# Gated recurrent attention with a small mixture of attention experts on one core: chunk 0's loads on two queues, zero products only at the start, a refitted order

## Chip, cores and metric

One core of a Trainium2 chip. The metric is the device time of one execution in microseconds (us); for the kernel before, the median of three runs is given. A difference within 0.2% (0.64 us) is about what a measurement of this kernel cannot tell from no change.

## What is computed

All inputs are float32: batch 4, 8 heads, 768 positions, head size 48, 4 experts of width 64.

```python
# stage 1, for every batch b and head h, over t:
state = alpha[t, :, None] * state + outer(k[t], v[t])    # 48 x 48
y[t] = q[t] @ state
# stage 2, x = y with the heads side by side, (4, 768, 384):
logits = x @ w_gate                                      # 4 experts, top 2, softmax over them
for e in range(4):
    q, k, v = x @ wq[e], x @ wk[e], x @ wv[e]
    a = causal_softmax(q @ k.T / sqrt(64))
    out += weight_of_expert_e * (a @ v @ wo[e])          # 0 where e is not chosen
```

## The kernel before

**Tiles and stages.** The positions of a batch are cut into 6 chunks of 128, so there are 24 chunks (n = 0 to 23); three chunks are a unit (u = 0 to 7), so a batch is two units. All 8 heads of a chunk are worked on together, as 4 pairs that lie on the 128 partitions.

For a chunk, VectorE first turns the decays into running products: `prep_r` (a scan and a reciprocal, operation `r`), `prep_c` (a second scan, `c`) and `prep_kq` (the multiplication of queries and keys by them, `kq`); GpSimd copies out the chunk's total decay (`e`). Chunk 0 is done in two pieces of two pairs each, so these carry a piece number: `r.0.0`, `r.0.1` and so on. TensorE then multiplies keys by queries (`gla_a`, L217, operation `a`), transposes the keys (`gla_t`, L234, `t`), forms the chunk's addition to the state (`gla_u`, L263, `u`) and the output (`gla_y`, L302, `y`), which sums the masked products of the chunk (`ms`) and the products with the state (`S`). Between them lie the mask (`m`, on VectorE L221, or on ScalarE L225 and GpSimd L229), the copies of the transposed keys (`kt`, `kr`, L238 or L240), and the state's own path: an addition on VectorE (L272), a scaling on GpSimd (L275) and the placing on ScalarE (L280).

For a unit, TensorE projects its 384 positions to queries and keys (`proj`, L325, `p`) and to values and gate logits (`vproj`, L351, `v`), forms scores (`score`, L400, `s`), transposes the weighted probabilities (`transp`, L452), multiplies them with the values (`av`, L477, `o`) and with `wo` (`outp`, L496, `w`). VectorE finds the maxima (L414, L407), ScalarE does the exponentials (L425), GpSimd the weighting (L437). Most matrices are split into a high and a low part, so that one product takes three passes (`xh` and `xl`, `wqkh` and `wqkl`). The low part of `wv` is made on TensorE by two products (L721, L722, operations `wx.v.0` and `wx.v.1`).

**What sets the order.** All instructions are written by a planner that runs while the kernel is built (`run`). It keeps a list of operations with what they depend on, the engines that may do them with an assumed duration each, the buffers they take, and a target time, which is a multiple of `PACE` (us for a chunk) with offsets from the table `OFF`. It goes through the engines in assumed time, takes for the engine that is next free the operation whose start and target are best (`PULL`, `HEAD`), and writes it down; the engines later run their instructions strictly in that order and wait on semaphores. `MARGIN` is added to the assumed time at which an input is there for TensorE. `FIRST` lists by hand the first operations of TensorE (P), VectorE (V), ScalarE (A) and GpSimd (G). `opening` issues the first loads and tells the planner when they are assumed to land (`arrive`, by `came`, from a rate and a lead).

**Zero products.** `warm` (L887) multiplies a constant tile with itself into an unused accumulator. `opening` writes four such products of 512 columns before any real work of TensorE. Later the planner writes more wherever it expects TensorE to be free for longer than `IDLE`:

```python
            if e == "P" and free["P"] > start and t - free["P"] > IDLE:
                x, i = min((s[0], i) for i, s in enumerate(slots["g"]) if s)
                k = int((t - max(x, free["P"]) - IDLE) / 0.11)
                if k > 0:
                    warm(i, k)
                    slots["g"][i] = [t, "P"]
```

The profile counts two records for each product of full-precision operands, such as these, those of L217, L263, L302 and L477, and one for each of the others.

**The first loads.** SyncE issues the decays of chunk 0 in two pieces (`load_al`, L118), ScalarE the queries and keys of chunk 0 in two pieces (`load_q`, L122); then SyncE issues the decays, queries and keys of chunks 1 and 2, the values, and the weights, in one long queue.

Of the kernel before, what the change touches and what calls it, by code (L numbers as in the profile page):

```python
# [17 lines left out]
B, H, S, D = 4, 8, 768, 48  # L18
# [8 lines left out]
P = 112  # L27
# [8 lines left out]
FIRST = dict(  # L36
    P="t.0 u.0 a.0 wx.v.0 a.1 t.1 wx.v.1 y.0 u.1",
    V="r.0.0 c.0.0 r.0.1 c.0.1 kq.0.0 kq.0.1 r.1.0 c.1.0 kq.1.0 r.2.0 m.1.1 m.1.0 S.1 c.2.0 kq.2.0 xl.0 sa.1 kt.2 xl.1 kr.2 m.2.1 m.2.0 r.3.0 c.3.0",
    A="kr.0 kt.0 wvh m.0.1 m.0.0 wl.v.0 kt.1 kr.1 B.1 wl.v.1 wqh.0 xh.0 xh.1 B.2 vo.0.0 wqh.1 xh.2 kt.3 vo.0.1 ph.0.0.0 ph.0.0.1 woh ck.0 vo.0.2 ck.2 kr.3 B.3",
    G="e.0.0 e.0.1 e.1.0 m.0.1 m.0.0")  # L40
RATE, LEAD = 377.0, 3.35
PACE = 12.4288
PULL = {"P": 0.0081, "V": 0.0044, "A": 0.0049, "G": 0.0171, "S": 0.0015}
SWITCH = 1.5202
# [5 lines left out]
CHANGE.update({(x, "f"): 0.2 for x in "asy"})  # L50
IDLE = 0.1929
SHARE = 0
HEAD = 0.012
MARGIN = 0.4162
SLOW = 1.1285
OFF = dict(load=2.5246, prep=0.6013, a=0.5833, y=-0.1718, p=0.0404, pw=0.5861, v=-0.6489, g=0.8219, s=-0.1513, step=0.9077, n=0.4583, tr=1.4644, o=1.0477, w=1.1357, wt=-1.0315, wv=-2.1607, hx=0.2944, hs=-1.4408, hp=1.0247, ck=0.1758, end=0.5579, hd=0.2767, sx=-0.9018, wo=-2.426, xo=0.3522, tk=-0.0639, kt=-0.2994, u=0.5172, m=-0.5537, ph=0.7581, vo=1.3685, to=0.0454, oh=-0.2153, rd=0.1911)
UNITS = dict(a=7, at=4, ms=2, kt=2, x=2, q=3, k=4, yy=2, vg=3, T=4, al=3, v=4, ot=2, st=2)
# [6 lines left out]
def tile_gla_moe(ctx: ExitStack, tc: tile.TileContext, qk_d, al_d, v_d, wqk_d, wv_d, wo_d, nat_d, vn_d, out_d):  # L64
# [486 lines left out]
    def chunk_ops(n):  # L551
# [12 lines left out]
        if not last:  # L564
            zt = (n - 1 + OFF["tk"] - head) * PACE
            op(("t", n), zt, [("kq", n, i) for i in range(len(pieces(n)))], [("P", 0.32, lambda: gla_t(n))], [("T", n)], [("pt", n), ("kt", n)], "t")
            zt += OFF["kt"] * PACE
            op(("kt", n), zt, [("t", n)], either(gla_k, 288, n), [("pt", n), ("kt", n)])
            op(("kr", n), zt, [("t", n)], either(gla_kr, 96, n), [("pt", n), ("kt", n)])
        z = (n + OFF["y"] - head) * PACE  # L570
# [5 lines left out]
        if not last:  # L576
            z = (n + OFF["u"] - head) * PACE
            op(("u", n), z, [("kt", n), ("kr", n), ("Lv", n)], [("P", 0.36, lambda: gla_u(n))], [("kt", n), ("v", n)], [("pu", n)], "y")
            nxt = [("e", n + 1, i) for i in range(len(pieces(n + 1)))]
            if n + 1 not in WHOLE:  # L580
                nxt.append(("cp", n + 1))
            z += (OFF["hs"] if n < HALF else OFF["sx"]) * PACE
            past = [("B", n - 1)] if n and c != 1 else []
            if c == 0:
                op(("S", n + 1), z, [("u", n)] + nxt + past, [("V", 0.37, lambda: state_first(n))], [("pu", n), ("T", n + 1)])
            else:
                op(("sa", n), z, [("u", n), ("S", n)], [("V", 0.37, lambda: state_add(n))], [("pu", n), ("st", n)], [("st", n)])
                op(("S", n + 1), z, [("sa", n)] + nxt + past, [("G", 0.6, lambda: state_scale(n))], [("st", n), ("T", n + 1)])
            op(("B", n + 1), z, [("S", n + 1)] + ([("y", n - 1)] if n else []), [("A", 0.62, lambda: state_place(n + 1))])

    def front_ops(u):
# [20 lines left out]
        back = [("g3", u - 1)] if u else []  # L612
        op(("g1", u), z, [("vo", u, 2)] + back, [("V", 0.87, lambda: gate_1(u))], [("vg", u)], lock=2)
        op(("g2", u), z, [("g1", u)], [("A", 0.21, lambda: gate_2(u))])
# [111 lines left out]
    def low_ops(name, z, done, w, high, low, n, wt):  # L726
        if name not in LOWS:
            f = lambda E: E.tensor_tensor(low, w, high.bitcast(F32), OP.subtract)
            op(("wl",) + name, z, [done], [("V", dv(n), lambda: f(V)), ("G", 0.12 + 0.0021 * n, lambda: f(G))], [wt], lock=True)
            return  # L730
# [36 lines left out]
    def run(start, arrive, busy):  # L767
# [37 lines left out]
        while todo:  # L805
# [86 lines left out]
    def opening():  # L892
# [26 lines left out]
        for n in (1, 2):  # L919
# [180 lines left out]
```

## Time and profile before

| | us |
|---|---|
| median of 3 runs (318.54 to 319.06) | 318.57 |
| the profiled execution | 318.76 |
| its span, first to last instruction | 317.0 |
| TensorE busy (weight loads beside it) | 308.2 (265.4) |
| VectorE busy | 249.5 |
| ScalarE busy | 208.9 |
| GpSimd busy | 128.2 |

The profiled execution is 1.76 us longer than its span and 0.19 us above the median. PE is TensorE, PEld its weight loads, DVE VectorE, ACT ScalarE, POOL GpSimd, SP SyncE; SPq and ACTq are the engines' DMA issues. A timeline row gives the start, the duration and the number of like instructions that follow each other; in brackets stands how long the engine was idle before and what ended that. The ends of matrix products are modelled, so the next product may start before the one ahead has ended; what an operation takes of TensorE's time is read from start to start. The granted clock is a share of 2.4 GHz, in the page's part 2 in tenths.

### The profile page before, as it was taken

The numbers are of one execution on the slowest core, as the hardware profiler recorded it, in microseconds if no ns is written. First come the engines' busy times: TensorE is split into PE (matmuls) and PEld (weight loads), VectorE is DVE, ScalarE is ACT, GpSimd is POOL, SyncE is SP. The second block draws the span as 40 slices with busy tenths as digits, with TensorE's granted clock in tenths as the row PEclk, the third lists the DMA queues.
The fourth block names the chain that finished last, engine by engine and source line by source line (L and its number), as shares of the span: only waits on it lengthen the run. The fifth ranks groups of instructions, "written<-read, shape, count | busy, mean of one in ns | idle before, by whom it ended". The sixth has DMA issues, their size and how long they took to land.

```text
span 317.0 us, 11044 instructions
## 1 busy us (share of the span) xinstructions
PE 308.2 (97%) x4410; PEld 265.4 (84%) x4410; DVE 249.5 (79%) x678; ACT 208.9 (66%) x588; POOL 128.2 (40%) x197
## 2 busy tenths in 40 slices
PE   8999999999999999999999999999999999999992
PEld 3699989898997979889997988889897988888692
DVE  5999899998999998898998989675865754487620
ACT  2464986796785868578775776655964765377841
POOL 6334137516463483526343226414280344033510
PEclk9999999999999999999999999999999999999998
DMA  7996275543526246524354334304100000102001
GB/s 246 389 377 192 70 233 184 156 125 93 158 71 193 84 108 179 146 66 119 106 170 94 117 84 153 90 8 136 41 2 2 3 2 25 53 0 77 2 30 60
DMA packets 26893, 35.21 MB, mean 111 GB/s; under 512 B 2288, under 2 KB 22864, under 8 KB 26832
## 3 DMA queue, kind: packets, MB, share of 16 engines
q1 hardware_dynamic: 26144, 33.69, 34.6%
q8 instruction: 37, 0.61, 0.8%
q10 hardware_dynamic: 688, 0.72, 0.7%
q14 instruction: 24, 0.20, 0.2%
HBM read 27.61 MB, written 4.72 MB: 102 GB/s over the span
## 4 chain that ended last, share of the span: by engine, by line
PE 95%; DMA 1%; DVE 1%; ACT 0%; issue 0%; ACTq 0%; DVEq 0%
PE g L325 16%; PE g L452 13%; PE g L477 12%; PE g L302 11%; PE g L400 11%; PE g L351 8%; PE g L496 8%; PE g L217 7%; PE g L887 3%; PE g L263 2%; PE g L234 2%; DMA at<-in_al_dram 1%; DVE at L178 1%; PE g L721 0%; DVE T L198 0%
## 5 line engine op out<-in xcount | busy, mean ns | idle before, releaser
L437 POOL TENSOR_SCALAR a<-a,cf,gw 128x128 f32<-128x128 f32 (+5 forms) x96 | 80.5, 851 | 71.4 <-DVE cf L431 45.5
L425 ACT ACTIVATE a<-a,mx 128x256 f32<-128x256 f32 (+3 forms) x96 | 51.5, 539 | 9.1 <-DVE mx L414 9.0
L452 PE MATMUL g<-ident,a 128*128 128x128 f32 x336 | 53.7, 277 | 0.0
L325 PE MATMUL g<-x,wqkh 128*128 128x384 f32 x192 | 51.7, 350 | 0.0
L229 POOL TENSOR_SCALAR_AFFINE_SELECT ms<-ms 128x512 f32<-128x512 f32 x31 | 22.1, 724 | 56.2 <-ACT ms L225 56.2
L452 PEld LDWEIGHTS g<-ident,a 128*128 128x128 f32 x336 | 39.7, 140 | 5.8 <-issue 2.3
L240 DVE COPY at<-g 128x512 f32<-128x512 f32 (+3 forms) x62 | 29.2, 479 | 16.9 <-PE g L452 15.9
L477 PE MATMUL g<-at,vg 128*32 128x384 f32 (+2 forms) x648 | 39.7, 389 | 0.0
L400 PE MATMUL g<-k,q 64*128 64x256 f32 (+3 forms) x384 | 39.2, 336 | 0.0
L238 ACT ACTIVATE at<-g 128x512 f32<-128x512 f32 (+3 forms) x66 | 30.4, 465 | 8.4 <-PE g L452 6.6
L477 PEld LDWEIGHTS g<-at,vg 128*32 128x32 f32 x648 | 19.3, 109 | 18.5 <-issue 15.3
L302 PE MATMUL g<-ms,v 128*32 128x128 f32 x768 | 33.0, 274 | 0.0
L325 PEld LDWEIGHTS g<-x,wqkh 128*128 128x128 f32 x192 | 33.0, 189 | 0.0
L400 PEld LDWEIGHTS g<-k,q 64*128 64x128 f32 x384 | 28.6, 185 | 5.2 <-issue 2.3
L325 PE MATMUL g<-x,wqkl 128*128 128x384 f32 x96 | 32.3, 337 | 0.0
L351 PE MATMUL g<-wvh,x 128*128 128x260 f32 x144 | 31.7, 296 | 0.0
L414 DVE CUSTOM_DVE_ANT_0 a<-g,cmask 128x128 f32<-128x128 f32 (+2 forms) x64 | 28.2, 483 | 2.0 <-PE g L400 1.8
L496 PE MATMUL g<-woh,yy 128*128 128x384 f32 x96 | 28.1, 351 | 0.0
L217 PE MATMUL g<-T 48*128 48x128 f32 x384 | 25.7, 275 | 0.0
L217 PEld LDWEIGHTS g<-T 48*128 48x128 f32 x384 | 24.0, 187 | 1.3 <-DVE T L198 0.4
L351 PEld LDWEIGHTS g<-wvh,x 128*128 128x128 f32 x144 | 24.0, 190 | 0.4 <-ACT ms L225 0.4
L302 PE MATMUL g<-T,S 112*32 112x128 f32 x480 | 24.2, 272 | 0.0
(113 smaller groups left out, 616.1 us busy)
## 6 DMA issues: line engine op xcount, KB each, us to landing
al<-in_al_dram SPq DMA_DIRECT2D x21, 387.0 KB, 3.9
T<-in_qk_dram SPq DMA_DIRECT2D x21, 384.0 KB, 4.2
v<-in_v_dram SPq DMA_DIRECT2D x24, 256.0 KB, 4.5
out_dram<-ot SPq DMA_DIRECT2D x23, 192.0 KB, 2.1
T<-T SPq DMA_DIRECT2D x42, 48.2 KB, 2.2
a<-in_al_dram SPq DMA_DIRECT2D x2, 516.0 KB, 6.7
T<-in_qk_dram SPq DMA_DIRECT2D x2, 512.0 KB, 7.1
at<-in_wqk_dram SPq DMA_DIRECT2D x1, 768.0 KB, 8.5
```

The lines of the kernel that those rows point to most:

```text
L217: PE.matmul(pa[s][:, C * p:C * p + C], t[r:r + D, p, C:2 * C], t[r:r + D, p, 0:C], start=True, stop=True, tile_position=(r, 0))
L238: A.activation(out, src, AF.Copy)
L240: V.tensor_copy(out, src)
L302: PE.matmul(o[32 * j:32 * j + 32, k], l, r, start=(i == 0), stop=(i == len(parts) - 1), tile_position=(0, 32 * j))
L325: PE.matmul(pj[:, :W3], w[:, kt, cs], x[:, kt, :], start=(i == 0), stop=(i == 8))
L351: PE.matmul(pv[:, 0:260], x[:, kt, 128 * i:128 * i + 128], w[:, kt, :], start=(m == 0), stop=(m == 8))
L400: PE.matmul(sc(u, pair, i, e, x, c1 - c0), q[r, i0, ts], k[r, i1, c0:c1], start=(y == 0), stop=(y == 2), tile_position=(64 * e, 0))
L425: A.activation(a[:, c0:c1], src, AF.Exp, bias=mx[:, 1:2], scale=-1.0 if last else 1.0, accum_out=sm[:, x:x + 1])
L437: G.tensor_scalar(a[:, 0:n], a[:, 0:n], CF[u % 2][:, 3 * pair + i, e:e + 1], gw[:, u, i, eg:eg + 1], op0=OP.mult, op1=OP.mult)
L452: PE.transpose(pt[:, 128 * (j - j0):128 * (j - j0) + 128], a[:, 128 * j:128 * j + 128], ident)
L477: PE.matmul(o[r:r + 32, lo:n1], v[:, j % 3, 64 * eg + x:64 * eg + x + 32], at(("at", u, pair, e))[:, min(j, 4), at_off(j) + lo:at_off(j) + ...
L496: PE.matmul(po[:, 0:DM], y[:, h, 128 * i:128 * i + 128], w[:, pair, :], start=(m == 0), stop=(m == 5))
```

## The change

1. The four loads of chunk 0 are issued ahead of all else, by ScalarE and SyncE in turn: decays piece 0 on ScalarE, piece 1 on SyncE, then queries and keys piece 0 on ScalarE, piece 1 on SyncE. The planner gets four fixed landing times for them in place of a rate.
2. The planner writes zero products only while its assumed time is below `START` = 27 and the assumed wait is over `IDLE` = 0.7; before, at any time and from 0.1929 on. The four products of `opening` stay.
3. Some assumed durations are corrected, and the planner's constants and the hand-written first order are set anew. What each instruction computes stays the same.

```diff
-    P="t.0 u.0 a.0 wx.v.0 a.1 t.1 wx.v.1 y.0 u.1",
-    V="r.0.0 c.0.0 r.0.1 c.0.1 kq.0.0 kq.0.1 r.1.0 c.1.0 kq.1.0 r.2.0 m.1.1 m.1.0 S.1 c.2.0 ...
+    P="a.0 t.0 u.0 wx.v.0 a.1",
+    V="r.0.0 r.0.1 c.0.0 kq.0.0 c.0.1 kq.0.1 r.1.0 c.1.0 kq.1.0 r.2.0 m.1.0 m.1.1 S.1 c.2.0 ...
...
-PACE = 12.4288
+PACE = 12.3704
...
-IDLE = 0.1929
+START = 27.0
+IDLE = 0.7
...
-MARGIN = 0.4162
+MARGIN = 0.4105
...
-            op(("kr", n), zt, [("t", n)], either(gla_kr, 96, n), [("pt", n), ("kt", n)])
+            op(("kr", n), zt, [("t", n)], either(gla_kr, 134, n), [("pt", n), ("kt", n)])
...
-                op(("S", n + 1), z, [("sa", n)] + nxt + past, [("G", 0.6, lambda: state_scale(n))], [("st", n), ("T", n + 1)])
-            op(("B", n + 1), z, [("S", n + 1)] + ([("y", n - 1)] if n else []), [("A", 0.62, lambda: state_place(n + 1))])
+                op(("S", n + 1), z, [("sa", n)] + nxt + past, [("G", 0.52, lambda: state_scale(n))], [("st", n), ("T", n + 1)])
+            op(("B", n + 1), z, [("S", n + 1)] + ([("y", n - 1)] if n else []), [("A", 0.75, lambda: state_place(n + 1))])
...
-            if e == "P" and free["P"] > start and t - free["P"] > IDLE:
+            if e == "P" and start < free["P"] < START and t - free["P"] > IDLE:
...
-        for i in (0, 1):
-            load_al(0, i, SY)
+        for load in (load_al, load_q):
+            for i, eng in enumerate((A, SY)):
+                load(0, i, eng)
         G.memset(ones, 1.0)
         A.activation(ones, ones, AF.Copy)
-        for i in (0, 1):
-            load_q(0, i, A)
...
-        for key, kb in (("La", 0, 0), 264), (("La", 0, 1), 264), (("Lq", 0, 0), 262), (("Lq", 0, 1), 262):
-            came(key, kb)
-        z[0] += 0.3
+        for key, us in (("La", 0, 0), 3.7), (("La", 0, 1), 4.7), (("Lq", 0, 0), 5.5), (("Lq", 0, 1), 6.2):
+            arrive[key] = (us, "S")
+        z[0] = 6.45
```

Two more assumed durations change in the same way (`gate_1` 0.87 to 0.96, the low parts of weights on GpSimd by 0.08), the whole table `OFF` and most of `PULL` get other numbers, and the first lists of ScalarE and GpSimd change in places. In the listings below the change's lines from 52 on are one higher than before, those of `opening` up to two.

TensorE at the start. `T_85` holds chunk 0's queries and keys, `v_92` its values, `kt_69` its transposed keys, `d1r` is the tile of the zero products. Before:

```order
L887 MATMUL g_108<-d1r 128x512 x4
L234 MATMUL g_101<-ident,T_85 128x128 x3
L887 MATMUL g_102<-d1r 128x512
L887 MATMUL g_102<-d1r 128x128
L263 MATMUL g_103<-v_92,kt_69 32x48 x3
```

In the change:

```order
L888 MATMUL g_108<-d1r 128x512 x4
L218 MATMUL g_101<-T_85 128x128
L218 MATMUL g_102<-T_85 128x128
L218 MATMUL g_101<-T_85 128x128
L218 MATMUL g_102<-T_85 128x128
L218 MATMUL g_101<-T_85 128x128
L218 MATMUL g_102<-T_85 128x128
L218 MATMUL g_101<-T_85 128x128
L218 MATMUL g_102<-T_85 128x128
L235 MATMUL g_103<-ident,T_85 128x128 x3
L888 MATMUL g_104<-d1r 128x384
L264 MATMUL g_105<-v_92,kt_69 32x48 x3
```

The products of keys and queries have moved ahead of the transposes, and the 640 columns of zeros behind the transposes are 384.

VectorE at the start (`at_63` holds chunk 0's decays, `a` those of chunk 1). Before:

```order
L178 SCALAR_TENSOR_TENSOR at_63<-at_63,d1r 128x258
L184 RECIPROCAL d1c_110<-at_63 128x2
L178 SCALAR_TENSOR_TENSOR at_63<-at_63,d1c_110 128x258
L178 SCALAR_TENSOR_TENSOR at_63<-at_63,d1r 128x258
L184 RECIPROCAL d1c_110<-at_63 128x2
L178 SCALAR_TENSOR_TENSOR at_63<-at_63,d1c_110 128x258
L198 TENSOR_TENSOR T_85<-T_85,at_63 128x2x2x128 x2
L178 SCALAR_TENSOR_TENSOR a<-a,d1r 128x516
```

In the change:

```order
L179 SCALAR_TENSOR_TENSOR at_63<-at_63,d1r 128x258
L185 RECIPROCAL d1c_110<-at_63 128x2
L179 SCALAR_TENSOR_TENSOR at_63<-at_63,d1r 128x258
L185 RECIPROCAL d1c_110<-at_63 128x2
L179 SCALAR_TENSOR_TENSOR at_63<-at_63,d1c_110 128x258
L199 TENSOR_TENSOR T_85<-T_85,at_63 128x2x2x128
L179 SCALAR_TENSOR_TENSOR at_63<-at_63,d1c_110 128x258
L199 TENSOR_TENSOR T_85<-T_85,at_63 128x2x2x128
L179 SCALAR_TENSOR_TENSOR a<-a,d1r 128x516
```

The same eight instructions stand ahead of chunk 1's first scan; the multiplication of the first piece has moved ahead of the second piece's second scan.

TensorE between the outputs of chunks 3 and 4 (`ms_67` and `ms_68` are their masked products, `S_114` and `S_115` their states). Before:

```order
L302 MATMUL g_104<-ms_67,v_92 32x128 x8
L302 MATMUL g_104<-T_85,S_114 32x128 x4
L887 MATMUL g_105<-d1r 128x448
L302 MATMUL g_106<-ms_68,v_93 32x128 x4
L302 MATMUL g_106<-T_86,S_115 32x128 x4
```

In the change:

```order
L303 MATMUL g_105<-ms_67,v_92 32x128 x8
L303 MATMUL g_105<-T_85,S_114 32x128 x4
L303 MATMUL g_107<-ms_68,v_93 32x128 x4
L303 MATMUL g_107<-T_86,S_115 32x128 x4
```

The 448 columns of zeros are gone. In all, 22 of the 27 zero products of the program are left out; TensorE's other products are the same in number and size, in an order that differs over the whole program. Apart from the zeros that order falls into 297 pieces of one kind each before (a piece being products of one kind that follow each other), and 292 now.

## Rows read from the trace of the kernel before

**Rows 1.** The page, parts 1 and 2: busy time by engine, granted clock in 40 slices.
```profile
PE 308.2 (97%) x4410; PEld 265.4 (84%) x4410; DVE 249.5 (79%) x678; ACT 208.9 (66%) x588; POOL 128.2 (40%) x197
...
PEclk9999999999999999999999999999999999999998
```

**Rows 2.** Waits of the whole run: who waited for whom, us in total, times, longest.
```profile
PE g L887 <- POOL d1r L151: 1.6, 1, 1.6
...
PE g L234 <- ACT ms L225: 0.4, 1, 0.4
```

**Rows 3.** Windows, all engines: stretch, its us, then busy us (x instructions) of each engine.
```profile
8.00:27.00 19.00, 18.25 (x344) 15.22 (x344) 18.18 (x27) 8.94 (x19) 7.56 (x10) 1.00 1.05 376
27.00:100.00 73.00, 72.59 (x1150) 64.61 (x1150) 67.06 (x176) 56.43 (x160) 33.00 (x48) 1.00 0.48 140
100.00:312.00 212.00, 210.92 (x2917) 183.03 (x2913) 160.18 (x470) 141.72 (x406) 82.18 (x113) 1.00 0.25 74
```

**Rows 4.** The same windows for line 887 (the zeros) alone.
```profile
8.00:27.00 19.00, 3.47 (x15) 2.23 (x14) 1.00 1.05 376
27.00:100.00 73.00, 3.35 (x12) 1.79 (x12) 1.00 0.48 140
100.00:312.00 212.00, 4.47 (x20) 3.05 (x20) 1.00 0.25 74
```

**Rows 5.** Timeline of TensorE, 41.6 to 46 us: start, us, engine, line, operation.
```profile
41.69 0.43 PE L887 MATMUL g<-d1r 128*128 128x64 f32 x2
41.93 0.37 PE L351 MATMUL g<-wvh,x 128*128 128x260 f32 x1
...
44.86 1.02 PE L887 MATMUL g<-d1r 128*128 128x448 f32 x2
45.81 0.42 PE L302 MATMUL g<-ms,v 128*32 128x128 f32 x8
```

**Rows 6.** Timeline of ScalarE, 44 to 45 us: the placing of a state.
```profile
44.35 0.73 ACT L280 ACTIVATE S<-sp 48x192 f32<-48x192 f32 x2
```

**Rows 7.** Timeline of the last unit, around 293 us.
```profile
293.01 0.86 ACT L238 ACTIVATE at<-g 128x512 f32<-128x512 f32 x2
...
293.11 0.81 PE L887 MATMUL g<-d1r 128*128 128x320 f32 x2
...
293.76 0.83 PE L452 MATMUL g<-ident,a 128*128 128x128 f32 x6
```

**Rows 8.** Timeline of the opening, 0 to 11 us.
```profile
1.58 6.42 PE L887 MATMUL g<-d1r 128*128 128x512 f32 x8 [1.58 <-POOL d1r L151]
...
4.74 0.70 DVE L178 TENSOR_TENSOR_SCAN at<-at,d1r 128x258 f32<-128x258 f32 x1 [2.73 <-DMA at<-in_al_dram]
...
7.84 1.27 DVE L198 TENSOR_TENSOR T<-T,at 128x512 f32<-128x512 f32 x2
...
8.61 0.88 PE L234 MATMUL g<-ident,T 128*128 128x128 f32 x3 [0.61 <-issue]
...
9.33 1.25 PE L887 MATMUL g<-d1r 128*128 128x512 f32 x4
...
10.50 0.54 PE L263 MATMUL g<-v,kt 128*32 128x48 f32 x32
```

**Rows 9.** DMA issues, 0.5 to 1.2 us: count, KB each, us from issue to landing.
```profile
at<-in_al_dram SPq DMA_DIRECT2D x1, 258.0 KB, 3.8
T<-in_qk_dram ACTq DMA_DIRECT2D x1, 256.0 KB, 2.7
```

**Rows 10.** DMA issue of chunk 2's decays, at 4.71 us.
```profile
a<-in_al_dram SPq DMA_DIRECT2D x1, 516.0 KB, 7.7
```

**Rows 11.** Timeline, 12.9 to 18.9 us: the chain of chunk 2.
```profile
12.91 1.66 DVE L178 TENSOR_TENSOR_SCAN a<-a,d1r 128x516 f32<-128x516 f32 x1
...
17.45 1.23 DVE L198 TENSOR_TENSOR T<-T,a 128x1024 f32<-128x1024 f32 x1
...
18.89 0.50 PE L234 MATMUL g<-ident,T 128*128 128x128 f32 x3
```

More of the change, by code (lines that the diff above doesn't have):

```diff
@@ L36 @@
 FIRST = dict(
-    P="t.0 u.0 a.0 wx.v.0 a.1 t.1 wx.v.1 y.0 u.1",
-    V="r.0.0 c.0.0 r.0.1 c.0.1 kq.0.0 kq.0.1 r.1.0 c.1.0 kq.1.0 r.2.0 m.1.1 m.1.0 S.1 c.2.0 kq.2.0 xl.0 sa.1 kt.2 xl.1 kr.2 m.2.1 m.2.0 r.3.0 c.3.0",
-    A="kr.0 kt.0 wvh m.0.1 m.0.0 wl.v.0 kt.1 kr.1 B.1 wl.v.1 wqh.0 xh.0 xh.1 B.2 vo.0.0 wqh.1 xh.2 kt.3 vo.0.1 ph.0.0.0 ph.0.0.1 woh ck.0 vo.0.2 ck.2 kr.3 B.3",
-    G="e.0.0 e.0.1 e.1.0 m.0.1 m.0.0")
+    P="a.0 t.0 u.0 wx.v.0 a.1",
+    V="r.0.0 r.0.1 c.0.0 kq.0.0 c.0.1 kq.0.1 r.1.0 c.1.0 kq.1.0 r.2.0 m.1.0 m.1.1 S.1 c.2.0 kq.2.0 xl.0 sa.1 kt.2 xl.1 kr.2 m.2.1 m.2.0 r.3.0",
+    A="kr.0 kt.0 wvh m.0.1 m.0.0 kr.1 wl.v.0 kt.1 B.1 xh.0 wl.v.1 wqh.0 xh.1 B.2 wqh.1 vo.0.0 xh.2 kt.3 vo.0.1 ph.0.0.0 ph.0.0.1 woh vo.0.2 ck.0 ck.2 ck.1 B.3 kr.3",
+    G="e.0.1 e.0.0 e.1.0 m.0.1 m.0.0")
 RATE, LEAD = 377.0, 3.35
-PACE = 12.4288
-PULL = {"P": 0.0081, "V": 0.0044, "A": 0.0049, "G": 0.0171, "S": 0.0015}
+PACE = 12.3704
+PULL = {"P": 0.0081, "V": 0.0043, "A": 0.0032, "G": 0.0196, "S": 0.001}
 SWITCH = 1.5202
@@ L50 @@
 CHANGE.update({(x, "f"): 0.2 for x in "asy"})
-IDLE = 0.1929
+START = 27.0
+IDLE = 0.7
 SHARE = 0
-HEAD = 0.012
-MARGIN = 0.4162
+HEAD = 0.0115
+MARGIN = 0.4105
 SLOW = 1.1285
-OFF = dict(load=2.5246, prep=0.6013, a=0.5833, y=-0.1718, p=0.0404, pw=0.5861, v=-0.6489, g=0.8219, s=-0.1513, step=0.9077, n=0.4583, tr=1.4644, o=1.0477, w=1.1357, wt=-1.0315, wv=-2.1607, hx=0.2944, hs=-1.4408, hp=1.0247, ck=0.1758, end=0.5579, hd=0.2767, sx=-0.9018, wo=-2.426, xo=0.3522, tk=-0.0639, kt=-0.2994, u=0.5172, m=-0.5537, ph=0.7581, vo=1.3685, to=0.0454, oh=-0.2153, rd=0.1911)
+OFF = dict(load=2.4221, prep=0.5384, a=0.5441, y=-0.1718, p=0.0259, pw=0.5861, v=-0.6489, g=0.7648, s=-0.1513, step=0.9077, n=0.3362, tr=1.3713, o=0.5352, w=1.2595, wt=-0.8102, wv=-2.1751, hx=0.2017, hs=-1.2056, hp=1.0247, ck=-0.2447, end=0.0443, hd=0.1404, sx=-0.8251, wo=-2.426, xo=0.3048, tk=-0.0836, kt=-0.0348, u=0.5172, m=-0.8441, ph=0.5776, vo=1.3513, to=0.1575, oh=-0.454, rd=0.2704)
 UNITS = dict(a=7, at=4, ms=2, kt=2, x=2, q=3, k=4, yy=2, vg=3, T=4, al=3, v=4, ot=2, st=2)
@@ L612, in front_ops @@
         back = [("g3", u - 1)] if u else []
-        op(("g1", u), z, [("vo", u, 2)] + back, [("V", 0.87, lambda: gate_1(u))], [("vg", u)], lock=2)
+        op(("g1", u), z, [("vo", u, 2)] + back, [("V", 0.96, lambda: gate_1(u))], [("vg", u)], lock=2)
         op(("g2", u), z, [("g1", u)], [("A", 0.21, lambda: gate_2(u))])
@@ L728, in low_ops @@
             f = lambda E: E.tensor_tensor(low, w, high.bitcast(F32), OP.subtract)
-            op(("wl",) + name, z, [done], [("V", dv(n), lambda: f(V)), ("G", 0.12 + 0.0021 * n, lambda: f(G))], [wt], lock=True)
+            op(("wl",) + name, z, [done], [("V", dv(n), lambda: f(V)), ("G", 0.2 + 0.0021 * n, lambda: f(G))], [wt], lock=True)
             return
```

## The prediction

> **What bounds the kernel now.** I read the page first: TensorE is busy for 97% of the span, and its granted clock is full (2.4 GHz) in all slices but the last [rows 1]. A busy TensorE need not be a useful one, so the view of waits came next. TensorE waited for another engine only at the very start and once later, for 0.4 us [rows 2]; everywhere else its next product had its inputs. So the end is set by the sum of what TensorE executes, zeros included. The windows say how close the others are: from 27 to 100 us VectorE is busy for 67.1 of 73 us, from 100 us on for 160 of 212 [rows 3]. VectorE is thus the second bound in the first third, and far from one later. The same windows for the zeros' line alone [rows 4] give what can be saved: 3.5 us busy from 8 to 27 us, 3.4 from 27 to 100, 4.5 from 100 on.
>
> **What a block of zeros costs.** Busy time overstates it, since modelled ends overlap. The 64 columns at 41.69 are busy for 0.43 us, but the next product starts 0.24 us later; the 448 columns at 44.86 are busy for 1.02 us and hold the next product up for 0.95 [rows 5]. I take 0.19 off for each block (two records), a little too much for the long ones. Was anything hidden under them? The output at 45.81 needs a state that ScalarE has placed by 45.08 [rows 6], and its masked products come first; without the zeros it could have begun at about 44.9. That block covered next to nothing. The one at 293.11 is of the other kind: the transposes behind it start at 293.76, and ScalarE is still copying from 293.01 to 293.87 [rows 7], so a part of its 0.65 is a real wait. Between all and nothing of it I take 0.4.
>
> **The opening.** Before, TensorE executes zeros until 8.00 (1.58 and 6.42), which the change keeps; VectorE starts its first scan at 4.74, when SyncE's first load has landed, ends the multiplications at 9.11 (7.84 and 1.27), and TensorE's first real product starts at 8.61 [rows 8]. ScalarE's first load, of the same size, took 2.7 us to land against SyncE's 3.8 [rows 9]. With the decays of piece 0 on ScalarE the first scan may begin 1.0 us sooner; the second then waits for the piece that SyncE brings, at 4.6 or 4.7. VectorE's eight instructions, 4.4 us in all, end at 8.2 to 8.4 in place of 9.1, and TensorE begins behind its zeros, at 8.0 at the soonest: 0.6 gained. Little of this lasts. Chunk 2's decays are issued at 4.71 and land 7.7 us later [rows 10], at 12.4, and VectorE already scans them at 12.91; from there one chain of VectorE runs to 18.68 (17.45 and 1.23), and chunk 2's transposes follow at 18.89 [rows 11]. So at that point **0.5** us is the most that is left, and I take it. For the same reason the zeros ahead of it, the 640 columns at 9.33 among them [rows 8], free nothing more: they hide behind that chain, and if the chain were shorter they would count. The 384 columns that stay lie in the same shade, and cost nothing.
>
> Against this gain speaks the Trainium skill, page "DMA: Bandwidth & Descriptors", section "Issuing engines are not separate DMA queues": transfers started by different engines share the same DMA engines, and starting them on several saves only the issuing engine's time. The rows agree that both queues share one stream, but show that ScalarE's first piece still came first; by the rule alone the 0.5 would be nothing, and the time half a microsecond longer.
>
> **The rest, by stage.**
> - 18.9 to 27 us: three blocks go (two of 64 columns, one of 192), some 0.24 each by [rows 5], 0.7. Chunk 2's output between them follows masked products that VectorE makes right after that chain, so I count **0.3**; the ends are 0 and 0.7.
> - 27 to 100 us: 12 records, 6 blocks: 3.35 less 6 times 0.19 is **2.2**.
> - 100 us to the end: 20 records, 10 blocks: 4.47 less 1.9 is 2.6; less 0.4 for the real wait at 293 and 0.2 for the last block, which stands behind the last product: **2.0**.
> - The refitted order: same products, 292 pieces in place of 297. The nearest price is a 64-column block, 0.24 for two changes of kind and the product [rows 5], so at most 1.2 either way; I take nothing.
> - The corrected durations cost nothing by themselves; they only steer that order.
>
> That is 5.0 us if nobody is late. Next in line is VectorE. At 100 us TensorE would be 3.0 us ahead of before (0.5, 0.3, 2.2), and VectorE must hand over its work as much sooner. It starts 0.5 sooner and has 5.9 us of idle time from 27 to 100 [rows 3]; 2.5 of these must vanish. Some do by themselves, since VectorE's idle time is partly waiting for products that now come sooner; the pauses between its 176 instructions don't. I take 1.7 of the 2.5, so **0.8** comes back as waits of TensorE. Sum: 4.2 us. From the profiled execution's 318.76 that is 314.56; the median lies 0.19 lower, so I predict **314.4**.
>
> **Rivals.**
> - *VectorE gives nothing.* All of its idle time stays, the 2.5 come back, and the gain is 2.5: 316.1. For it: 92% busy. Against it: its waits are partly for TensorE.
> - *The clock falls.* In the opening TensorE now has short pauses in place of zeros, for the copies of the keys and for the weights' landing. The page grants the full clock from the first slice on [rows 1], yet the opening's 2048 columns of zeros take 6.42 us, 1.6 for 512, and the 640 columns at 9.33 only 1.17 to the next product, 0.94 for 512 [rows 8]: most of the first stretch ran at half the rate, as at 1.2 GHz. One more such stretch of 6 us would cost 3: 317.4. Against it: the pauses are about as long as the 0.4 us wait of [rows 2], beside which the clock stayed full. [...]
> - *The waits return where the zeros stood.* If the zeros hid what the planner thought they hid, only the 0.5 of the opening is gained: 318.1, no change that can be measured. For it [rows 7], against it [rows 6].
> - *Slower: the state's path.* An output needs the state from VectorE, GpSimd and ScalarE in turn. At 46 us the state was ready at 45.08 and was used only after 45.81 [rows 5, 6]: with the 0.95 of zeros gone no reserve is left. TensorE takes its products strictly in order, so one late state holds up all behind it. A wait of 0.25 for each of the 20 states undoes the 5.0; at 0.35 it is 7.0, and the time 320.5.
>
> **The numbers.** The forecast gets 0.56, VectorE's rival 0.20, the clock 0.07, the returning waits 0.08, the slower one 0.09. The first three are faster by over 0.2% (0.64 us, about what a measurement of this kernel can tell from no change): 0.83; the fourth is the same: 0.08; the fifth slower: 0.09. The low end takes the 5.0 without the give-back, the other 0.4 before 27 us, and the 1.2 of a better order: 318.57 less 6.6, about 312.0. The high end takes in the returning waits, 318.2; left out is the slower case.
>
> **What will show it.** Right, if line 887 has ten records in place of 54, the clock stays full from 7 us on, TensorE's first real product starts near 8.0 and chunk 2's transposes near 18.4, and waits of TensorE for VectorE appear between 20 and 100 us, 1 to 3 us in all, with VectorE busier there than 92%. VectorE's rival shows as 3 us and more of such waits; the state's path as waits of L302 for ScalarE's L281 at many chunks. I am wrong in kind if TensorE's products, without zeros, take longer than before, or if the granted clock falls; wrong in size if the waits in 20 to 100 us are far from 1 to 3.

## The result, and the profile after the change

Measured in turns on one chip, the kernel before takes 318.57 us again, and the change **315.13 us** (median of four: 313.15, 313.94, 316.33, 318.19); the ratio is 0.987, with a 95% interval of 0.984 to 0.990. That is inside the range, 0.7 above the forecast. What the forecast did not see is the spread: 5 us, where the kernel before keeps within 0.6 here and within 1.7 on any chip below. The profiled execution of the change is its slowest, the 318.19, which the ratio leaves out (the other three have a median of 313.94); so what follows rests on it only where a second profile or the times of other runs say the same.

The page answers to [rows 1]; TensorE's share has fallen by a point, and one slice of the granted clock is no longer full:

```profile
PE 305.2 (96%) x4366; PEld 262.2 (83%) x4366; DVE 248.2 (78%) x680; ACT 207.5 (66%) x586; POOL 125.2 (40%) x195
...
PEclk9999999899999999999999999999999999999999
```

The waits of TensorE, against [rows 2]: 3.4 us for SyncE's copies of key rows (T<-T), and 0.8 for VectorE.

```profile
PE g L218 <- DMA T<-T: 3.4, 3, 1.6
PE g L888 <- POOL d1r L152: 1.6, 1, 1.6
PE g L218 <- DVE T L199: 0.8, 2, 0.6
```

The windows of [rows 3], then those of [rows 4] for the zeros (now line 888), whose 8 records of the start and 2 of 10 us are all that is left. From 27 to 100 us VectorE is busy for 62.6 of 73 us, **less** than before: it was not pressed harder, it was held up.

```profile
8.00:27.00 19.00, 18.06 (x338) 14.48 (x337) 18.63 (x29) 8.62 (x20) 8.94 (x11) 1.00 1.06 380
27.00:100.00 73.00, 68.93 (x1087) 63.03 (x1085) 62.61 (x164) 55.00 (x156) 30.78 (x45) 0.98 0.47 138
100.00:312.00 212.00, 211.91 (x2937) 182.07 (x2937) 162.75 (x480) 141.71 (x408) 79.71 (x114) 1.00 0.25 73
```

```profile
0.00:8.00 8.00, 6.08 (x8) 2.37 (x8) 1.00 0.75 238
8.00:27.00 19.00, 0.81 (x2) 0.30 (x2) 1.00 1.06 380
```

The timeline of TensorE shows where. Line 218 makes the products of keys and queries of a chunk, 16 records that take 1.05 to 1.16 us in one piece. For chunk 5 they begin at 38.89 and end with a wait for the copies at 41.76; for chunk 6 there are two such waits, to 51.74 and 53.06.

```profile
38.89 1.28 PE L218 MATMUL g<-T 48*128 48x128 f32 x14
41.76 0.48 PE L218 MATMUL g<-T 48*128 48x128 f32 x2 [1.60 <-DMA T<-T]
...
49.89 0.84 PE L218 MATMUL g<-T 48*128 48x128 f32 x12
51.74 0.48 PE L218 MATMUL g<-T 48*128 48x128 f32 x2 [1.01 <-DMA T<-T]
53.06 0.48 PE L218 MATMUL g<-T 48*128 48x128 f32 x2 [0.83 <-DMA T<-T]
```

Right behind it the clock falls to 1.2 GHz; the windows show a busy TensorE at half the full rate for 3.4 us:

```profile
54.20:57.60 3.40, 3.40 (x15) 3.40 (x14) 1.58 (x3) 1.87 (x7) 0.63 (x1) 0.50 0.00 0
```

The copies stand in SyncE's queue behind bulk loads. In the change, chunk 5's go out 0.7 us sooner than before, but two loads now follow at once; chunk 6's, which went out at 45.99 before, stand behind a load of queries and keys (line 123) that leaves only at 46.77, when TensorE's products have freed its buffer. First SyncE's timeline of the change, then that of before:

```profile
35.00 0.60 SPq L119 DMA_DIRECT2D al<-in_al_dram  x1
35.70 1.21 SPq L204 DMA_DIRECT2D T<-T  x2
37.00 1.28 SPq L119 DMA_DIRECT2D al<-in_al_dram  x2
...
45.23 0.38 SPq L123 DMA_DIRECT2D T<-in_qk_dram  x1
45.66 0.48 SPq L126 DMA_DIRECT2D v<-in_v_dram  x1
46.77 0.38 SPq L123 DMA_DIRECT2D T<-in_qk_dram  x1
47.25 1.31 SPq L204 DMA_DIRECT2D T<-T  x2
```

```profile
35.73 0.60 SPq L118 DMA_DIRECT2D al<-in_al_dram  x1
36.43 1.76 SPq L203 DMA_DIRECT2D T<-T  x2
38.28 0.60 SPq L118 DMA_DIRECT2D al<-in_al_dram  x1
...
45.41 0.48 SPq L125 DMA_DIRECT2D v<-in_v_dram  x1
45.99 1.31 SPq L203 DMA_DIRECT2D T<-T  x2
```

At line 204 the copies land 2.1 to 5.1 us after their issue, 2.2 in the median; at line 203 before it was 2.1 to 4.2 (the last row of the view of one line, first the change, then before):

```profile
DMA to landing us min/median/max: 2.1/2.2/5.1
```

```profile
DMA to landing us min/median/max: 2.1/2.2/4.2
```

The planner takes 2.2 for every one of them, the median; the corrected durations of the change left that number alone. For chunks 5 and 6, whose copies go out from 35 to 49 us among dense loads, 2.2 is too little: chunk 6's took 5.1 here, and those of the two chunks 3.6 to 4.2 before.

The opening, against [rows 8, 9, 11], in the timeline and the DMA issues: the two first loads leave at once, and land 3.8 and 4.5 us later. VectorE's first scan begins at 4.67, TensorE's first product at 7.74, chunk 2's transposes (line 235) at 18.64.

```profile
4.67 0.70 DVE L179 TENSOR_TENSOR_SCAN at<-at,d1r 128x258 f32<-128x258 f32 x1 [2.66 <-DMA at<-in_al_dram]
...
5.49 0.67 DVE L179 TENSOR_TENSOR_SCAN at<-at,d1r 128x258 f32<-128x258 f32 x1
...
7.74 0.72 PE L218 MATMUL g<-T 48*128 48x128 f32 x8
...
9.07 0.72 PE L218 MATMUL g<-T 48*128 48x128 f32 x8 [0.62 <-DVE T L199]
...
18.64 0.55 PE L235 MATMUL g<-ident,T 128*128 128x128 f32 x3
```

```profile
at<-in_al_dram SPq DMA_DIRECT2D x1, 258.0 KB, 4.5
at<-in_al_dram ACTq DMA_DIRECT2D x1, 258.0 KB, 3.8
T<-in_qk_dram ACTq DMA_DIRECT2D x1, 256.0 KB, 4.6
T<-in_qk_dram SPq DMA_DIRECT2D x1, 256.0 KB, 5.3
```

And the end, which no row ahead of the prediction showed. In the kernel before, TensorE's last semaphore instructions (line 1096, PEldq) begin at 316.6, 1.8 us behind ScalarE's (ACTq) of the same step; in the change both are at 315.9. The view is that of the line, in which the two numbers at the end are the first and the last start: before, then the change.

```profile
L1096 ACTq EVENT_SEMAPHORE  x2: 17/17/17, 314.8 to 317.0; - x2
...
L1096 PEldq EVENT_SEMAPHORE  x2: 51/51/51, 316.6 to 317.0; - x2
```

```profile
L1096 ACTq EVENT_SEMAPHORE  x2: 17/17/17, 315.9 to 316.4; - x2
...
L1096 PEldq EVENT_SEMAPHORE  x2: 51/51/51, 315.9 to 316.4; - x2
```

From the issue of the last store to the end of the span this is 5.7 us before (311.30 to 317.0) and 3.9 after (312.53 to 316.5). So the profiled execution of the change issues its last store 1.2 us **later** than before, and is faster all the same.

### The profile page after: what moved, and what is told of

Same layout as the page of the kernel before. It is cut to its first block, busy times and chain, and to the rows that moved or that the text cites. A ratio compares the mean times of both kernels' runs of the same rounds, so it can differ in the third digit from the quotient of the medians.

```text
span 316.5 us, 10944 instructions
## 1 busy us (share of the span) xinstructions
PE 305.2 (96%) x4366; PEld 262.2 (83%) x4366; DVE 248.2 (78%) x680; ACT 207.5 (66%) x586; POOL 125.2 (40%) x195
## 4 chain that ended last, share of the span: by engine, by line
PE 82%; DVE 8%; DMA 5%; issue 2%; POOL 1%; SPq 0%; ACT 0%; POOLq 0%; DVEq 0%; ACTq 0%
PE g L326 14%; PE g L453 13%; PE g L478 12%; PE g L401 11%; PE g L303 8%; PE g L497 8%; PE g L352 7%; PE g L218 5%; DMA T<-T 3%; DVE al L179 2%; DVE T L199 2%; PE g L264 2%; PE g L235 2%; DMA at<-in_al_dram 1%; DVE a L179 1%
## 5 line engine op out<-in xcount | busy, mean ns | idle before, releaser
L438 POOL TENSOR_SCALAR a<-a,cf,gw 128x128 f32<-128x128 f32 (+5 forms) x96 | 76.1, 805 | 72.5 <-DVE cf L432 49.3
L230 POOL TENSOR_SCALAR_AFFINE_SELECT ms<-ms 128x512 f32<-128x512 f32 x29 | 20.6, 724 | 75.2 <-ACT ms L226 75.2
L241 DVE COPY at<-g 128x256 f32<-128x256 f32 (+3 forms) x63 | 29.7, 481 | 18.5 <-PE g L453 17.6
L239 ACT ACTIVATE at<-g 128x512 f32<-128x512 f32 (+3 forms) x65 | 29.3, 467 | 7.8 <-PE g L453 7.1
L326 PEld LDWEIGHTS g<-x,wqkh 128*128 128x128 f32 x192 | 33.7, 192 | 0.3
L352 PE MATMUL g<-wvh,x 128*128 128x260 f32 x144 | 32.5, 301 | 0.0
L218 PE MATMUL g<-T 48*128 48x128 f32 x384 | 27.2, 276 | 4.4 <-DMA T<-T 3.4
L218 PEld LDWEIGHTS g<-T 48*128 48x128 f32 x384 | 24.7, 187 | 7.0 <-DMA T<-T 4.0
```

The lines of the kernel that those rows point to most:

```text
L218: PE.matmul(pa[s][:, C * p:C * p + C], t[r:r + D, p, C:2 * C], t[r:r + D, p, 0:C], start=True, stop=True, tile_position=(r, 0))
L239: A.activation(out, src, AF.Copy)
L241: V.tensor_copy(out, src)
L326: PE.matmul(pj[:, :W3], w[:, kt, cs], x[:, kt, :], start=(i == 0), stop=(i == 8))
L352: PE.matmul(pv[:, 0:260], x[:, kt, 128 * i:128 * i + 128], w[:, kt, :], start=(m == 0), stop=(m == 8))
L438: G.tensor_scalar(a[:, 0:n], a[:, 0:n], CF[u % 2][:, 3 * pair + i, e:e + 1], gw[:, u, i, eg:eg + 1], op0=OP.mult, op1=OP.mult)
```

## The experiments

They ran in three groups, each with the kernel before in turns on its chip; the three chips differ by up to 0.4 us there (medians 318.72 for e0 to e3, 318.30 for f1 to f4, 318.69 for g1 to g4), which belongs to any comparison across groups. The theory: the zeros gave 4 us, and late copies, with the clock that falls behind them, take a part back in some runs. The rivals: VectorE gives nothing; the zeros had kept the clock up; the opening gains nothing.

**e0: the change once more.** No instruction differs.

> The changed kernel once more, instruction for instruction (its plan is only written down first and issued afterwards), as the yardstick for the next three and to see what its runs vary by. Theory (late copies): chunks 5 and 6 wait in the middle of their key products for SyncE's two small copies, 2 us and more each, TensorE idles, and its clock falls to half for some 3 us behind it. How late the copies land differs from run to run, so times spread over 313 to 317, and the profile of a quicker run shows smaller waits in these two places and less or no half clock. Rival (VectorE bounds it): runs agree within 1 us, and waits for VectorE outweigh those for the copies.

Median 316.12 of eight, from 313.81 to 318.43; ratio 0.993 (0.990 to 0.995). The profile is of the quickest, and has no wait for the copies; TensorE's second group of waits is for VectorE, 0.69 at 45.31, where chunk 6's transposes need keys that VectorE is still multiplying:

```profile
38.78 1.16 PE L218 MATMUL g<-T 48*128 48x128 f32 x16
...
45.31 0.55 PE L235 MATMUL g<-ident,T 128*128 128x128 f32 x3 [0.69 <-DVE T L199]
...
48.42 1.45 PE L218 MATMUL g<-T 48*128 48x128 f32 x16
```

```profile
27.00:60.00 33.00, 32.29 (x539) 29.21 (x539) 31.33 (x82) 27.11 (x78) 16.86 (x24) 1.00 0.57 162
```

VectorE is busy for 31.3 of 33 us from 27 to 60. So the quick run is the one that the prediction described, with a give-back of VectorE of about its size (0.69 for 0.8; its sign, 1 to 3 us of such waits, is not reached), and the slower ones are another matter. The mean granted clock of the runs says where part of their time went: 0.997 in the run of 313.81, 0.990 and 0.991 in those of 316.58 and 316.53, 0.986 in that of 318.43. It is not all: one of 315.79 has a full clock.

**e1: the zeros alone.** The kernel before; the order of every engine stays:

```diff
-                    warm(i, k)
+                    if free["P"] < START:
+                        warm(i, k)
```

> The kernel before, with every block of zeros after 27 us left out and nothing else moved: VectorE, ScalarE, GpSimd and SyncE have the same order. The working of the prediction makes this 2.2 and 2.0 us, 314.4, if nobody is late. Theory (late copies): in the kernel before the copies for chunks 5 and 6 landed only 0.28 and 0.63 us ahead of their use, and some 0.6 and 1.7 us of zeros go ahead of these two places, so about 1.1 to 1.4 come back as waits for the copies: 315.5 (315.0 to 316.0), with waits for VectorE under 1 us. Rival (VectorE gives nothing): 316.5 and more, with waits for VectorE of 2 us. Rival (zeros kept the clock): the granted clock falls between 27 and 100 us, and the time is 317 or more.

314.59 (314.10 to 315.56); ratio 0.988 (0.986 to 0.990). One condition is, by the medians, 1.5 faster than the whole change on the same chip; the runs overlap (three of e0's eight are within e1's range or below it), so what the runs show is that it is no slower. The rows say how it comes about: TensorE's last product of the program's own starts at 307.61 in place of 310.36.

```profile
310.36 0.34 PE L496 MATMUL g<-woh,yy 128*128 128x384 f32 x1
```

```profile
307.61 0.34 PE L496 MATMUL g<-woh,yy 128*128 128x384 f32 x1
```

Of these 2.75, and 0.3 more that its opening lost, 1.5 come ahead of 102 us and 1.6 behind it; the rest is the end, 3.9 us in place of 5.7. No wait for VectorE or the copies stands in its list, though chunk 5's key products take 1.47. Neither rival holds, nor does the theory's own 315.0 or more: the copies gave back 0.4 at most. What came back, came elsewhere. The 448 columns at 44.86 had held TensorE up for 0.95 [rows 5]; without them e1 is 1.8 us ahead of before at the output that follows, where it had been 0.7 ahead until then, but by 48 us it is 0.5 ahead. ScalarE places the state at 44.26, hardly sooner than before (44.35, [rows 6]), behind its exponentials, and TensorE waits (TensorE's timeline, then ScalarE's):

```profile
44.66 0.69 PE L302 MATMUL g<-T,S 112*32 112x128 f32 x5 [0.22 <-ACT S L280]
```

```profile
44.26 0.74 ACT L280 ACTIVATE S<-sp 48x192 f32<-48x192 f32 x2
```

**e2: the change with zeros.** Blocks again wherever the plan has a gap of over 0.19 us:

```diff
-            if e == "P" and start < free["P"] < START and t - free["P"] > IDLE:
+            idle = IDLE if free["P"] < START else 0.1929
+            if e == "P" and start < free["P"] and t - free["P"] > idle:
```

> The changed kernel, with zeros put back after 27 us wherever its plan has a gap of over 0.19 us, as before (22 blocks, 2560 columns, against 17 blocks and 2176 columns there); no other instruction moves. Theory (late copies): the plan does not know that the copies are late, so hardly a block stands at the two waits; the blocks cost 4 to 5.5 us, the waits shrink by up to 1 since TensorE comes later, and the time is 3.5 to 5 above the change: 318.5 to 320. Rival (the zeros fill real gaps in the new order): at most 1.5 above the change. Rival (zeros hold the clock up): no fall of the clock behind 50 us, and at most 2 above.

318.35 (ratio 0.998, 0.997 to 1.000), 2.2 above e0: between theory and rival. In the order of the change the zeros cost half of what they cost before (4.1 by e1), likely since part of them fills waits; one wait for the copies is left, 0.66 at 41.86. The clock stays up (0.994 and more in all twelve runs, most at 0.997 to 1.000), so they may also do what the last rival says, and buy back part of their price.

**e3: the old loads in the change.**

```diff
-        for load in (load_al, load_q):
-            for i, eng in enumerate((A, SY)):
-                load(0, i, eng)
+        for i in (0, 1):
+            load_al(0, i, SY)
...
+        for i in (0, 1):
+            load_q(0, i, A)
```

> The changed kernel, with chunk 0's four loads as before: both pieces of the decays on SyncE, both of the queries and keys on ScalarE behind its first activation. No other instruction moves. The prediction said 0.5 us: by it this is 0.5 slower, first real product 0.6 later, chunk 2's transposes 0.5 later. The trace of the change says less: chunk 2's transposes came 0.25 sooner than before and the loads behind the first four landed 0.35 later. If two queues only push the stream back, chunk 2's decays land at 12.4 again in place of 12.7 and its transposes no later than 18.6: this is then 0 to 0.3 faster, or the same. The runs of the change vary by more than that, so the opening of the profile decides, not the time.

316.73 (ratio 0.993, 0.991 to 0.996), 0.6 above e0: the prediction's size, but within the scatter of twelve runs from 314.08 to 318.75. The profile decides: the first product starts at 8.58 in place of 7.68 (e0), chunk 2's transposes at 19.45 in place of 18.10. VectorE's first scan began at 4.74, 5.05 and 4.95 with the old loads (before, e1, e3) and at 4.67, 4.17 and 4.50 with the new (the change, e0, e2): 0.5 sooner on average. With the profiles of f1 to g4 it is ten with the new loads, 4.06 to 4.79, and four with the old, 4.74 to 5.05: still 0.5 by the means, with a scatter of its own that is larger. The two queues are worth something; how much at the end, this run cannot say.

**f1: copies ahead of loads**, in SyncE's queue, for chunks 5 and 6 alone:

```diff
+ SyncE: copies(5)  load decays(6)      ...  copies(6)  load q,k(9)
- SyncE: load decays(6)  copies(5)      ...  load q,k(9)  copies(6)
```

> The changed kernel with two swaps in SyncE's queue and nothing else moved: the copies of chunk 5 go ahead of the load of chunk 6's decays, those of chunk 6 ahead of the load of chunk 9's queries and keys, which had waited for TensorE to free the buffer. Theory (late copies): the copies have some 0.4 to 0.5 MB less ahead of them in the stream, about 1 us, and chunk 6's are issued up to 0.5 sooner, so a late run waits 1 to 2 us less in these two places and the clock stays full: median 1 to 2 below the change as measured in the first four (316.1), that is 314 to 315, and a spread under 3 us in place of 4.6. Rival (the whole stream lags, not its order): same median within 0.7, same spread.

314.36, and all four runs within 313.54 to 314.73; ratio 0.987 (0.985 to 0.990). Four of the twelve runs of the change (the first four and e0) are as quick as that; the rest reach to 318.43. No wait for a copy is left, and the clock is 0.997 or more in each run; TensorE waits 1.55 for VectorE at 46.36 instead. That is what the theory expected, and the trace shows the step between: chunk 5's two copies land 2.2 to 2.4 us after their issue, chunk 6's 2.2, where even the quick run e0 has 3.1 to 3.6 and up to 3.8 (the last row of the view of line 204 from 34 to 44 us, f1, then e0):

```profile
DMA to landing us min/median/max: 2.2/2.3/2.4
```

```profile
DMA to landing us min/median/max: 3.1/3.3/3.6
```

For chunk 5 this is a new order and not the old one: in the kernel before, too, its copies stood behind chunk 6's decays. It was another chip than e0's, on which the kernel before takes 0.4 less, the unchanged change did not run there, and there are four runs; so some 1.3 of the 1.8 between the medians is left as a size, and that the spread is the copies' alone is not proved.

**f2: copies on ScalarE's queue.** `SY.dma_start` becomes `A.dma_start` in `spread`, nothing else.

> The changed kernel with all 42 copies issued by ScalarE in place of SyncE, at the same places of the plan; no other order moves. Theory (late copies behind bulk loads of one queue): on a queue with nothing else in it they land in at most 3.5 us, against up to 5.1 now, and the waits of chunks 5 and 6 go. But ScalarE pays some 0.6 us for each issue and stands still until VectorE has multiplied: 25 us more in all, most of it while it is idle (207 of 316 us busy). If nobody waits for it, 313.5 to 315; if TensorE then waits for ScalarE's copies and exponentials, 317 and more. Rival (queues do not matter, the engines that move data are shared): landings as long as now.

321.60 (ratio 1.011, 1.009 to 1.012). The copies do land sooner than in e0, those of chunk 5 in 2.2 us (3.1 to 3.6) and of chunk 6 in 2.9 to 3.4 (up to 3.8), with 2.2 in the median of all as ever: another queue helps them here, as the theory says. The longest of all is 3.8, more than the 3.5 expected, and as long as the longest of e1 on SyncE's queue. ScalarE loses more by issuing them in its own order of work: TensorE now waits for it in five places, 3.1 us in all, up to 1.1 each. The rest of the 5.5 above e0 (on another chip) was not followed up.

**f3: the planner told the truth.** `land=2.2` becomes `land=4.5` for the copies, and the plan is made anew.

> The changed kernel planned anew with one number corrected that the change left alone: the copies are taken to land 4.5 us behind their issue in place of 2.2 (the longest landings in the trace are 4.2 before and 5.1 in the change). Theory (late copies): the planner then puts other products ahead of the key products of chunks 4 to 7, no wait for copies is left, and the runs agree within 2 us; the whole order moves, and is no longer fitted, which may cost 1 to 3: 314 to 318. Rival (VectorE): the spread stays and waits for VectorE remain the largest group.

315.44, all four within 314.93 to 315.62; ratio 0.991 (0.989 to 0.992). In these four runs the spread goes with this one number, and no wait for copies is left; the order that was not fitted anew costs about 1 against f1. The rival falls: its waits for VectorE are 1.0 us in all.

**f4: e1 with the new loads.** The diff of e3 the other way round, in the kernel before without its later zeros.

> The kernel before without the zeros after 27 us (314.59 in the first four) and with the change's four loads of chunk 0, one of each kind on either queue; the orders of the five engines are else those of before. In the profiles so far VectorE's first scan began at 4.74, 5.05 and 4.95 with the old loads and at 4.67, 4.17 and 4.50 with the new, 0.47 sooner by the means. If the opening passes this on to the end: 314.1 (313.7 to 314.4). If chunk 1 and 2's loads then land as much later: 314.6. The copies wait more often the sooner TensorE comes, which would give back up to 0.5.

313.95 (313.55 to 314.66); ratio 0.987 (0.985 to 0.989). It is the best median of the study, with two parts of the change, and without its order. Against f1, on the same chip, the fitted order, even with its copies put ahead, is worth nothing that can be told (313.95 to 314.36). Against e1 the new loads give 0.6 by the medians and 0.2 once the chips are set against each other; in the profiles the last product starts 0.55 sooner (307.06 to 307.61).

**g1: the kernel before, a second profile.**

> The kernel before, once more, for a second profile. In the first one 5.7 us passed between the issue of the last store (311.30) and the end of the span; in the kernel before without its later zeros it was 4.0, in the change 3.9 to 4.2, in the change with zeros put back 4.5. About 1.5 us of what the profiles show between before and change thus lie behind the last product. If that belongs to the kernel before, it is there again, 5.5 or more; if it is chance, 4.0 to 4.5, and the span is 315.5. Theory (late copies): the key products of chunks 5 and 6 take about 1.06 again, with no wait for the copies over 0.3.

318.92. From the last store's issue (311.24) to the end (317.1) it is 5.9 us again, and TensorE's last semaphore is again 1.8 us behind ScalarE's (316.8 and 315.0). The slow end belongs to the kernel before. Chunk 5's key products take 1.07.

**g2: f4 with chunk 5's copies first.**

> The kernel before less the zeros after 27 us, with the new loads (313.95), and chunk 5's copies ahead of chunk 6's decays in SyncE's queue, as was worth 1.8 us in the change. Nothing else moves. There chunk 5's key products take 1.46 in place of 1.06 and chunk 6's waited 0.2, so at most 0.6 is to be had: 313.4 to 313.9. Rival (nothing waits behind these two places): the same within 0.3, since the 0.4 is made up by a wait further on.

316.24 (ratio 0.992, 0.990 to 0.993): **2.3 slower** than f4 (1.9 if the 0.4 between their chips is taken off), which nobody expected. The load that was put behind the copies brings chunk 6's decays; it leaves at 37.78 in place of 35.14, and in this order VectorE scans them at once. VectorE waits 1.79 for them, and TensorE twice 0.84 (VectorE's timeline, then TensorE's):

```profile
41.37 0.96 DVE L178 TENSOR_TENSOR_SCAN al<-al,d1r 128x387 f32<-128x387 f32 x1 [1.79 <-DMA al<-in_al_dram]
```

```profile
43.13 0.43 PE L302 MATMUL g<-ms,v 128*32 128x128 f32 x8 [0.84 <-DVE mx L414]
...
46.02 0.70 PE L302 MATMUL g<-T,S 112*32 112x128 f32 x5 [0.84 <-ACT S L280]
```

So there is no rule that copies go first. Both are due at the same time there, and their order in the queue decides which is late.

**g3: g2 without the zeros between 9 and 27 us.** The condition of e1 becomes `if False`; the 2048 columns of the start stay.

> As g2, with the six records of zeros between 9 and 27 us left out as well (the 640 columns at 9.33 and four blocks of 64), so that only the 2048 columns of the start stay. By the prediction they lie in the shade of VectorE's chain: 0.3 sooner from the blocks behind 18.9, nothing from those ahead: 313.2 to 313.7, or the same. Rival (zeros hold the clock): TensorE then pauses for over 1 us at 9 to 11 and at 16 to 18 us, the granted clock falls there, and this is 1.5 to 3 slower than g2.

319.14, twelve runs from 317.22 to 321.03: 2.9 slower than g2. That is the rival's size, and in most runs its sign. The mean granted clock is below 0.994 in ten of the twelve (0.976 in the slowest run), 0.992 to 1.000 in g2, and never below 0.994 in 23 runs of the kernel before on this chip. But the profile is of the quickest run, with a full clock, and that run is 1.3 slower than g2's profiled one all the same; there the cost is a wait of 1.15 that the profile gives to no engine (the 1.72 at 10.54 costs nothing: with the zeros in g2 the same products started at 10.53). So some 1.3 of the 2.9 need no fall of the clock, and for the rest the runs' clocks speak, without a trace of such a fall.

```profile
10.54 0.54 PE L263 MATMUL g<-v,kt 128*32 128x48 f32 x32 [1.72 <-DMA v<-in_v_dram]
...
21.11 0.49 PE L217 MATMUL g<-T 48*128 48x128 f32 x3 [1.15 <-issue]
```

That wait stands in the middle of chunk 2's key products, whose inputs are all there as far as the profile shows. A 16 KB transfer of instructions lies ahead of it, from 18.64 to 19.70; in g2 the like one had ended by 17.99. Whether TensorE waited for its instructions was not tried.

**g4: f1 without the first zeros.** `warm(7, 32)` is left out.

> The change with the copies first (314.36), without the 2048 columns of zeros that open the program; 384 columns at 10 us stay. The zeros end at 8.0 and the first product waits for VectorE until then anyway, so they cost nothing; what they buy is the clock. In the change the granted clock rose at 6.4, behind 4.8 us of zeros. Without them TensorE's first products start at half the rate at 7.7, and the clock rises only some 5 us of work later: the products between 8 and 13 us, 3.5 us of work at the full rate, take twice as long, of which VectorE's chain to 18.1 hides a part: 0.5 to 3 slower, 315 to 317.5. Rival (the chain hides all of it, or the clock rises at once): the same within 0.4.

316.27 (315.57 to 317.68), 1.9 above f1, or 1.5 with the 0.4 between the chips taken off. The first products run at half the rate, 2.56 us for 16 records in place of 1.16, and the trace's record of a full clock begins only at 13.5 us, against 7.64 in f1. Products of zeros that nobody waits for bought 1.5 to 1.9 us.

```profile
7.63 2.56 PE L218 MATMUL g<-T 48*128 48x128 f32 x16 [7.63 <-DVE T L199]
```

## Why the prediction was right, and where it was not

- *The zeros, 2.2 and 2.0.* Right in kind, too large: e1 has 1.5 (0.3 of it the block at 25.35 us, so 1.2 from 27 to 100) and 1.6 on TensorE. Most of the first shortfall is one block: that the 448 columns at 44.86 "covered next to nothing" was misread, since TensorE comes sooner there than ScalarE places the state. That the whole came out at 4.1 in e1's median is luck: about 1.8 us more came from the end of the program, which the prediction did not look at: 5.7 and 5.9 us behind the last store's issue in the two profiles of before, 3.9 to 4.5 in all but one of the others (f3, 5.3, where that store lands late). The real wait at 293 [rows 7], set at 0.4, is 0.56 in e1.
- *The opening, 0.5.* Right in size: chunk 2's transposes come 0.25 (the change), 0.79 (e0) and 0.62 (e2) ahead of [rows 11], and 0.26 (f4) and none (g2, 18.91) in the order of before. Its reason was half wrong. ScalarE's load does not land in 2.7 us once SyncE's leaves at the same moment; in the ten profiles with the new loads the two land 3.1 to 3.8 and 3.9 to 4.6 after their issue, one behind the other. That fits what the Trainium skill says of shared engines ("DMA: Bandwidth & Descriptors", section "Issuing engines are not separate DMA queues"). By the rule alone nothing would be gained; the traces show about 0.5 at VectorE's first scan.
- *18.9 to 27 us, 0.3.* It is 0.6, near the end of 0.7: e0 is 0.8 ahead at the transposes and 1.4 at 25 us.
- *VectorE's give-back, 0.8.* The wait is there where it was foretold, 0.69 in e0 and 1.55 in f1, with VectorE at 95% from 27 to 60 us in e0. But it belongs to the order of the change: e1 and f4, as fast, have no such wait. In e1 what came back, about 1.2 at 44 to 48 us, goes with waits for ScalarE's state and GpSimd's weighting (0.22 and 0.24).
- *The refitted order, nothing, at most 1.2.* **This is the step that failed.** The prediction priced the order by TensorE's pieces alone and did not follow SyncE's queue. Chunk 6's copies had moved behind a load that waits for a buffer, and chunk 5's products 1.8 us ahead (from 40.70 to 38.89) of copies that leave only 0.7 sooner. In a good run nothing of it shows; the profiles of e2 and e3 have 0.7 and 0.8 us of such waits, and that of the change has 3.4, and 3.4 us at half the clock behind them, some 1.7 more. These 5.1 are of the size of the 4.4 us between the change's two profiled spans (316.5 and 312.1). f1 puts both chunks' copies ahead, they land in 2.2 to 2.4 us, and the runs draw together. That makes late copies the likeliest source of most of the 1.3 to 1.8 us between its median and e0's; the slow runs themselves, but for the first, have no trace.
- *The clock.* The text called a fall of the clock "wrong in kind", gave it 0.07, and looked for it in the opening. It fell at 54 us, behind three waits of 0.8 to 1.6. g4 shows that the opening is as tender: the zeros of the start, which the change keeps, are worth 1.5 to 1.9 us. Those from 9 to 27 us, in the order of before, are worth 2.9 by g3, part of it with a full clock. The prediction had put these in the shade of VectorE's chain, where they cost nothing; it did not see that leaving them out could cost something. The Trainium skill's page "TensorE: Matmul & The Clock Gate", section "Why this matters for your kernels", asks for no idle gaps between bursts, but the gaps that it speaks of are longer than any wait between products in these traces. The fall at 54 us came behind waits of 1.60, 1.01 and 0.83 within 13 us, with TensorE at work between them, while g3's profiled run kept its clock with single waits of up to 1.72. Without their later zeros e1 and f4 hold the clock (0.996 and more in every run); behind 27 us TensorE has no wait over 0.6 there.
- *Returning waits, and the state's path.* Neither came as a rule. e1's only wait for a placed state is the 0.22 at 44.66, the place that the prediction had named.

So the sum came out near the median partly by luck: the zeros gave less than forecast and the late copies took some of it back, while the end of the program, which the forecast had left out, gave 1.8.

What stays open: why the copies land late in some runs of the change and not in others, what TensorE's last instructions wait for in the kernel before, and what the 1.15 us in g3 are.

## What to carry to other kernels

Read a moved order on the queues first: for each transfer that is moved, what stands ahead of it, what that waits for, and how far ahead of its use it lands, in the densest stretch and not in the median. A small reserve in one trace can be a wait in the next order, and where the engine behind it idles, a fall of its clock can add half as much again, as here 1.7 us behind 3.4 of waits. In this kernel filler work was worth its time only where the engine would otherwise really stand still, as in the opening; elsewhere take it out, by itself, before the order is fitted again. And price each block by the engine that delivers the next input, not by its length: one block of 0.95 us gave almost nothing here.

## What the hardware showed that was not expected

- A copy of 48 KB lands 2.1 to 2.2 us after its issue in the median and up to 5.1 behind loads, on SyncE's queue (the change); f1's order brings the copies of chunks 5 and 6 down to 2.2 to 2.4 on the same queue.
- The last steps of the program are 1.8 us late on TensorE alone in both profiles of the kernel before, and in none of the twelve others. In both, a 16 KB transfer of instructions ends 1.2 to 1.5 us ahead of them, and one ends 1.4 ahead of the end of g3's wait of 1.15. The queue that brings them moves 0.61 MB of instructions before, the only other one 0.20, and TensorE has 8820 of the program's 11,044 records, so it is most likely TensorE's; that it waits for them was not tried.
- Without the zeros of the start the record of a full clock begins at 13.5 us, 5.9 us after TensorE's first product; with them, in the thirteen other profiles, between 4.9 and 7.6.
